# Retention, a rational-gate layer and a gated layer on one core: the steady stages set in program order on every engine

## Chip, core and metric

The kernel runs on one core of a Trainium2 chip. The metric is the device time of one execution in microseconds (us). TensorE is called PE here, VectorE DVE, ScalarE ACT, GpSimd POOL and SyncE SP, as in the profile; PEld is TensorE's loading of weights.

## What is computed

```python
# retention, 4 x 8 heads, 576 positions, 64 wide; gamma per head
ret = (q @ k.T / sqrt(64)) * where(rel >= 0, gamma ** rel, 0)
x = (ret @ v)                       # 2304 tokens x 512
# layer 1: 512 -> 2048 -> 512, a rational gate
h = x @ w_in
P = a[0] + a[1]*h + a[2]*h**2 + a[3]*h**3
Q = 1 + abs(b[0])*abs(h) + abs(b[1])*h**2
x = (P / (Q + 1e-6)) @ w_out
# layer 2: 512 -> 1536 -> 512, rms norm, gated
xn = x / sqrt(mean(x*x) + 1e-6) * rms_g
g, val = xn @ w_gate, xn @ w_val
out = (g * sigmoid(g) * val) @ w_out2
```

The weights come as 64-bit floats. Each float32 factor is split into a high part and a rest, and every product is made of three products of such parts.

## The kernel before

**Head.** The retention, the conversion of layer 1's weights and layer 1's first 18 stages follow a list, `PLAN`, whose order is fixed on every engine by `in_order` (L636): it chains each instruction to the one before it on its engine. What is issued after the list is put in order by a scheduler that works from a modelled timeline.

**Layer 1.** Six tiles of 384 tokens, 16 stages each, one per 128 columns of the hidden width. `s` counts the stages, `n, j = divmod(s, 16)` gives tile and column block. Stage `s` is issued as follows. `m1_up(s)` (L368) makes 12 matmuls into bank 4 or 5. `m1_el` (L466) works on three stages at a time: for `s` ACT makes abs (L403), q (L406) and u (L412), POOL multiplies (`el_qq`, L419), DVE makes `el_p1` and `el_p2` (L423, L427), the last reader of the bank; for `s-1` ACT makes the reciprocal (L434, L439); for `s-2` DVE makes three steps (L443, L447, L452), ACT the high part of the gate's result (`el_gh`, L458) and POOL the rest (`el_gl`, L462). `m1_down(s-3)` (L380) adds the product with w_out into banks 0 to 3: eight matmuls on the high part, then four on the rest (L389).

**Side work in the stages.** A dictionary `late` holds pieces that go ahead of a stage. For the next tile: loads of x and their split (`x_load`, `x_split`, ACT L295 and POOL L299). For the tile that has ended (`be_plan`, L608): the banks are copied out (`be_evac`), squared and added (`be_sq`, L497), summed over partitions by a matmul with ones (`be_sum`, L508), the root is improved by three DVE instructions (`be_newton`, L519), x is scaled by four more (`be_xn`, L528) and stored (`be_out`). In the last tile four `wb.step` calls convert layer 2's weights: on ACT `high` (L194), `scale_hi` (L172), `scale_lo` (L180), on DVE `low` (L198), `shift` (L184), `add` (L190). They stand under `tc.issue_after(mark["el"].ins)`, which keeps them behind the latest activation of the stage.

**Layer 2.** `m2_up(nb, j)` (L539) makes 24 matmuls into banks 4 (gate) and 6 (value); ACT takes the Silu (L552), DVE multiplies (L553), ACT and DVE split the result (L555, L556); `m2_down` (L559) adds three products in each of three banks. Tiles 0 and 1 go side by side while the remaining weights are converted (`step_b`, which also takes a piece of the last tile's norm from the list `norm`), then tiles 2 to 5. With the last `j` the banks are copied out, on DVE, ACT and DVE, and stored through SP's queue (L570 to L574).

**Tables of ACT.** The first activation (L632) is `Abs`; a table is loaded before an activation whose function the active table lacks. Before, there are 7 loads: at L632, twice at L434, three times at L552, once at L513.

Of the kernel before, what the change touches and what calls it, by code (L numbers as in the profile page):

```python
# [12 lines left out]
ACTF = mybir.ActivationFunctionType  # L13
# [63 lines left out]
def retention_moe_kernel(  # L77
# [284 lines left out]


    acc = [b[:, 0:TA] for b in banks[0:KD]]
    g_t, el, el_t, mark = {}, {}, {}, {}
    NS = NA * J1

    def m1_up(s, part=None, b=None):  # L368
# [128 lines left out]
    def be_sq(n, m):  # L497
        if m == 0:
            ss = be_p.tile([128, TA], F32, tag="ss", name="ss")
            be[n] = (be[n], ss)  # L500
            act.activation(out=ss, in_=be[n][0][:, 0], func=ACTF.Square)
        else:
            x2, ss = be[n]
            sq = be_p.tile([128, TA], F32, tag="sq", name="sq")
            act.activation(out=sq, in_=x2[:, m], func=ACTF.Square)
            pool.tensor_tensor(out=ss, in0=ss, in1=sq, op=ALU.add)

    def be_sum(n):  # L508
        x2, ss = be[n]
        pt = banks[6][:, 0:TA]  # L510
        pe.matmul(out=pt, lhsT=ones, rhs=ss, start=True, stop=True)
        y = be_p.tile([128, TA], F32, tag="sq", name="y")
        act.activation(out=y, in_=pt, func=ACTF.Abs_reciprocal_sqrt, scale=1.0 / DM, bias=cst[:, 1:2])  # L513
        dve.tensor_scalar(
            out=ss, in0=pt, scalar1=-0.5 / DM, scalar2=-0.5 * EPS, op0=ALU.mult, op1=ALU.add
        )
        be[n] = (x2, ss, y)

    def be_newton(n):  # L519
        x2, ss, y = be[n]  # L520
        dve.tensor_tensor(out=ss, in0=ss, in1=y, op=ALU.mult)
        dve.tensor_tensor(out=ss, in0=ss, in1=y, op=ALU.mult)
        dve.scalar_tensor_tensor(out=ss, in0=ss, scalar=1.5, in1=y, op0=ALU.add, op1=ALU.mult)
        be[n] = (x2, ss)

    def be_xn(n, m):
        x2, r = be[n]
        dve.scalar_tensor_tensor(  # L528
            out=x2[:, m], in0=x2[:, m], scalar=rg[:, m:m + 1], in1=r, op0=ALU.mult, op1=ALU.mult
        )  # L530

    def be_out(n):
        sp.dma_start(out=xn_d[:, :, n * TA:(n + 1) * TA], in_=be.pop(n)[0])


    y_t = {}
    TT = TB // 128

    def m2_up(nb, j):  # L539
        x = x_t[NA + nb]  # L540
        ps = []
        for kind, b in (("g", 4), ("v", 6)):
            w = wb.got[kind, j]
            t = banks[b][:, 0:TB]
            for k in range(KD):
                ks = slice(k * 128, k * 128 + 128)
                pe.matmul(out=t, lhsT=w[:, 0, ks], rhs=x[:, 0, k], start=(k == 0), stop=False)  # L547
                pe.matmul(out=t, lhsT=w[:, 0, ks], rhs=x[:, 1, k], start=False, stop=False)  # L548
                pe.matmul(out=t, lhsT=w[:, 1, ks], rhs=x[:, 0, k], start=False, stop=(k == KD - 1))  # L549
            ps.append(t)  # L550
        sg = t_p.tile([128, TB], F32, tag="ah", name="sg")
        mark["el"] = act.activation(out=sg, in_=ps[0], func=ACTF.Silu)  # L552
        dve.tensor_tensor(out=sg, in0=sg, in1=ps[1], op=ALU.mult)  # L553
        y = g_p.tile([128, 2, TB], F32R, tag="g", name="y")
        act.activation(out=y[:, 0], in_=sg, func=ACTF.Copy)  # L555
        dve.tensor_tensor(out=y[:, 1], in0=sg, in1=y[:, 0].bitcast(F32), op=ALU.subtract)  # L556
        y_t[nb, j] = y

    def m2_down(nb, j):  # L559
        w, y = wb.got["o", j], y_t.pop((nb, j))  # L560
        for t in range(TT):
            ts = slice(t * 128, t * 128 + 128)
            a = banks[((0, 1, 2), (3, 5, 7))[nb % 2][t]]
            pe.matmul(out=a, lhsT=y[:, 0, ts], rhs=w[:, 0], start=(j == 0), stop=False)  # L564
            pe.matmul(out=a, lhsT=y[:, 0, ts], rhs=w[:, 1], start=False, stop=False)  # L565
            pe.matmul(out=a, lhsT=y[:, 1, ts], rhs=w[:, 0], start=False, stop=(j == J2 - 1))  # L566
            if j == J2 - 1:
                ob = o_p.tile([128, DM], F32, tag="ob", name="ob")
# [163 lines left out]
    x_load(xn_d, 1, 0)  # L732
    x_load(xn_d, 1, 1)
    x_split(NA + 1, 0)
    x_load(xn_d, 1, 2)
    x_split(NA + 1, 1)
    x_load(xn_d, 1, 3)
    m1_down(NS - 2)
# [10 lines left out]
    norm += [lambda: be_sum(NA - 1), lambda: be_newton(NA - 1)]  # L749
    norm += [lambda m=m: be_xn(NA - 1, m) for m in range(KD)]  # L750
    norm += [lambda: be_out(NA - 1)]

    def step_b(eng):
        if norm:
            norm.pop(0)()
        if not norm and len(extra) == 2:
            be_ctx.close()
            extra.extend([new_pool("wr", 2, "right")] * 2)
        if wb.n2 < len(b_order):
            with tc.issue_after(mark["el"].ins):  # L760
                wb.step(eng)

    def next_x(nb, j, j0):
        if nb < NBB and 0 <= j - j0 <= KD:
# [3 lines left out]
                x_load(xn_d, nb, j - j0)  # L768

    for j in range(1, J2):  # L770
        m2_up(0, j)
        if j == J2 - 1:
            o_p = new_pool("ob", 3, "right")
            next_x(2, 0, 0)
            x_load(xn_d, 2, 1)
        step_b(dve)
        m2_down(1, j - 1)
        step_b(dve)
        if j == J2 - 1:
# [4 lines left out]
        m2_up(1, j)  # L784
        step_b(dve)
        m2_down(0, j)
    last = (1, J2 - 1)
    for nb in range(2, NBB):
        for j in range(J2):
            next_x(nb + 1, j, 3)  # L790
            m2_up(nb, j)
            m2_down(*last)
            last = (nb, j)
    m2_down(*last)
# [76 lines left out]
```

## Time and profile before

| | |
|---|---|
| runs shown | 959.3 us median of 3 (957.12 to 961.98) |
| profiled execution, its own time | 957.84 us |
| its span | 956.1 us |
| PE busy | 932.5 us of the span, 5850 matmuls |
| DVE, ACT, POOL busy | 527.5, 530.9, 307.6 us |
| mean DMA rate | 82 GB/s; over 270 GB/s until 125 us |

The profile's page gives these. Matmuls overlap in it: a start follows the last by less than a matmul's own duration, so the distance between starts, not the duration, tells the pace. Of an idle time the view names what ended it.

### The profile page before, as it was taken

How to read it: one execution, taken by the hardware profiler on the slowest of the kernel's cores; microseconds unless marked ns; L12 is line 12 of the kernel's file. 1: busy time of each engine (PE TensorE's matmuls, PEld its weight loads, DVE VectorE, ACT ScalarE, POOL GpSimd, SP SyncE). 2: the span in 40 equal slices, each digit the busy share in tenths (PEclk: the TensorE clock that was granted, in tenths of full speed). 3: DMA queues.
4: the chain of work that ended last, by engine and by line, in shares of the span. 5: the costliest groups of instructions: out<-in, count | busy, mean ns of one | idle time of the engine just before them, and what ended most of it. 6: DMA issues, size and time to landing. Idle time of an engine off the chain costs nothing. (4 is left out here: it accounts for less than half of the span.)

```text
span 956.1 us, 14961 instructions
## 1 busy us (share of the span) xinstructions
PE 932.5 (98%) x5850; PEld 880.7 (92%) x5850; DVE 527.5 (55%) x967; ACT 530.9 (56%) x1030; POOL 307.6 (32%) x293
## 2 busy tenths in 40 slices
PE   7899999999999999999999999999999999999997
PEld 5788889999999999999899899999999999999996
DVE  5989988767767857767865755543112112112111
ACT  3877789779679678788786655533112112111111
POOL 5556756547457466465451000002001001000000
PEclk9999999999999999999999999999999999999999
DMA  9888962001010000010123544403002001000000
GB/s 327 290 280 287 327 204 94 1 34 34 15 36 17 34 25 10 34 34 24 55 86 103 165 132 132 132 31 124 1 1 67 1 1 50 1 1 34 1 1 34
DMA packets 37336, 77.92 MB, mean 82 GB/s; under 512 B 5520, under 2 KB 21008, under 8 KB 37264
## 3 DMA queue, kind: packets, MB, share of 16 engines
q1 hardware_dynamic: 37120, 76.95, 24.2%
q8 instruction: 46, 0.75, 0.3%
q14 instruction: 26, 0.21, 0.1%
q10 hardware_dynamic: 144, 0.01, 0.0%
HBM read 63.57 MB, written 13.37 MB: 80 GB/s over the span
## 5 line engine op out<-in xcount | busy, mean ns | idle before, releaser
L547 PE MATMUL bank<-x,w 128*128 128x384 f32 x528 | 177.0, 336 | 2.7 <-ACT sg L552 1.7
L549 PE MATMUL bank<-x,w 128*128 128x384 f32 x528 | 177.1, 336 | 0.0
L548 PE MATMUL bank<-x,w 128*128 128x384 f32 x528 | 176.8, 335 | 0.0
L553 DVE TENSOR_TENSOR sg<-sg,bank 128x384 f32<-128x384 f32 x72 | 39.9, 554 | 217.5 <-PE bank L549 214.0
L299 POOL TENSOR_TENSOR x<-xr,x 128x384 fp32r<-128x384 f32 x44 | 46.4, 1067 | 289.6 <-ACT x L295 288.3
L376 PE MATMUL bank<-x,w 128*128 128x384 f32 x384 | 131.1, 341 | 7.3 <-DVE u L427 3.0
L552 ACT ACTIVATE sg<-bank 128x384 f32<-128x384 f32 x72 | 35.4, 491 | 180.5 <-PE bank L549 180.5
L385 PE MATMUL bank<-g,w 128*128 128x384 f32 x384 | 129.8, 340 | 0.0
L378 PE MATMUL bank<-x,w 128*128 128x384 f32 x384 | 129.1, 336 | 0.0
L377 PE MATMUL bank<-x,w 128*128 128x384 f32 x384 | 128.9, 336 | 0.0
L386 PE MATMUL bank<-g,w 128*128 128x384 f32 x384 | 127.9, 334 | 0.0
L419 POOL TENSOR_TENSOR q<-q,ah 128x384 f32<-128x384 f32 x88 | 91.0, 1034 | 95.5 <-ACT q L406 92.7
L547 PEld LDWEIGHTS bank<-x,w 128*128 128x128 f32 x528 | 99.1, 188 | 6.5 <-ACT sg L552 2.1
L462 POOL TENSOR_TENSOR g<-u,g 128x384 fp32r<-128x384 f32 x80 | 82.7, 1035 | 59.8 <-issue 40.5
L548 PEld LDWEIGHTS bank<-x,w 128*128 128x128 f32 x528 | 99.1, 188 | 2.7
L549 PEld LDWEIGHTS bank<-x,w 128*128 128x128 f32 x528 | 99.1, 188 | 0.1
L555 ACT ACTIVATE y<-sg 128x384 fp32r<-128x384 f32 x72 | 37.6, 522 | 101.7 <-DVE sg L553 101.7
L423 DVE TENSOR_TENSOR u<-u,bank 128x384 f32<-128x384 f32 x96 | 52.9, 551 | 62.4 <-ACT u L412 60.5
L389 PE MATMUL bank<-g,w 128*128 128x384 f32 x384 | 86.7, 338 | 0.0
L376 PEld LDWEIGHTS bank<-x,w 128*128 128x128 f32 x384 | 72.4, 188 | 11.4 <-DVE u L427 4.7
L434 ACT ACTIVATE bank<-q,cst 128x384 f32<-128x384 f32 x96 | 56.0, 584 | 41.4 <-POOL q L419 34.9
L385 PEld LDWEIGHTS bank<-g,w 128*128 128x128 f32 x384 | 72.2, 188 | 1.2
(99 smaller groups left out, 1905.1 us busy)
## 6 DMA issues: line engine op xcount, KB each, us to landing
raw<-in_w_out_dram SPq DMA_DIRECT2D x28, 512.0 KB, 3.6
xb<-in_qkT_dram SPq DMA_DIRECT2D x16, 512.0 KB, 6.8
kv<-in_kv_dram SPq DMA_DIRECT2D x16, 512.0 KB, 6.1
raw<-in_w_in_dram SPq DMA_DIRECT2D x16, 512.0 KB, 5.4
raw<-in_w_gate_dram SPq DMA_DIRECT2D x12, 512.0 KB, 4.3
raw<-in_w_val_dram SPq DMA_DIRECT2D x12, 512.0 KB, 3.5
xn_d<-x SPq DMA_DIRECT2D x6, 768.0 KB, 3.8
xr<-xn_d SPq DMA_DIRECT2D x24, 192.0 KB, 2.4
```

The source lines that it names most:

```text
L376: pe.matmul(out=h, lhsT=w[:, 0, ks], rhs=x[:, 0, k], start=(k == 0), stop=False)
L377: pe.matmul(out=h, lhsT=w[:, 0, ks], rhs=x[:, 1, k], start=False, stop=False)
L378: pe.matmul(out=h, lhsT=w[:, 1, ks], rhs=x[:, 0, k], start=False, stop=(k == KD - 1))
L385: pe.matmul(out=acc[m], lhsT=w[:, 0, ms], rhs=g[:, 0], start=(j == 0), stop=False)
L386: pe.matmul(out=acc[m], lhsT=w[:, 1, ms], rhs=g[:, 0], start=False, stop=False)
L389: pe.matmul(out=acc[m], lhsT=w[:, 0, ms], rhs=g[:, 1], start=False, stop=(j == J1 - 1))
L419: eng.tensor_tensor(out=q, in0=q, in1=el_t[i]["ah"], op=ALU.mult)
L434: act.activation(out=el[i], in_=el_t[i]["q"], func=ACTF.Abs_reciprocal_sqrt, bias=cst[:, 0:1])
L462: eng.tensor_tensor(out=g[:, 1], in0=el_t[i]["r"], in1=g[:, 0].bitcast(F32), op=ALU.subtract)
L547: pe.matmul(out=t, lhsT=w[:, 0, ks], rhs=x[:, 0, k], start=(k == 0), stop=False)
L548: pe.matmul(out=t, lhsT=w[:, 0, ks], rhs=x[:, 1, k], start=False, stop=False)
L549: pe.matmul(out=t, lhsT=w[:, 1, ks], rhs=x[:, 0, k], start=False, stop=(k == KD - 1))
```

## The change

The stages from `S0` on are issued in the order in which the program lists them, on every engine, up to the last `j` of layer 2's first two tiles (`in_order(pinned)`), and once more for the last `m2_down`. A second dictionary, `done`, holds pieces that go behind a stage's `m1_el` instead of ahead of it: the splits of x, the squares, the Newton step, the scalings of x (one a stage) and the store. `tc.issue_after` is gone. `be_sum` is cut in two, the matmul and `be_root`. Layer 2's first x tile is loaded and split ten stages earlier. `m2_up` is cut into matmuls (`m2_mm`) and the rest (`m2_el`), and the very first value product goes to bank 5 instead of 6, so that all of tile 0's first product can stand ahead of layer 1's last three `m1_down`. The last tile's sum and root move to a fixed place in `j == 2`. The first activation asks for the reciprocal root's table. The last 128 rows of the output are copied and stored in two halves, by ACT and ACT's queue and by DVE and SP's.

```diff
@@ be_sum
         pe.matmul(out=pt, lhsT=ones, rhs=ss, start=True, stop=True)
+        be[n] = (x2, ss, pt)
+
+    def be_root(n):
+        x2, ss, pt = be[n]
         y = be_p.tile([128, TA], F32, tag="sq", name="y")
@@ m2_up
-    def m2_up(nb, j):
+    def m2_mm(nb, j):
-        for kind, b in (("g", 4), ("v", 6)):
+        for kind, b in (("g", 4), ("v", 6 if nb + j else 5)):
...
+        mm_t[nb, j] = ps
+
+    def m2_el(nb, j):
+        ps = mm_t.pop((nb, j))
...
@@ m2_down
+                r0 = nb * TB + t * 128
+                if nb == NBB - 1 and t == TT - 1:
+                    h = DM // 2
+                    act.activation(out=ob[:, 0:h], in_=a[:, 0:h], func=ACTF.Copy)
+                    dve.tensor_copy(out=ob[:, h:], in_=a[:, h:])
+                    act.dma_start(out=out[r0:r0 + 128, 0:h], in_=ob[:, 0:h])
+                    sp.dma_start(out=out[r0:r0 + 128, h:], in_=ob[:, h:])
+                    continue
@@ x_plan
-            late.setdefault(s0 + k + 1, []).insert(0, lambda k=k: x_split(to, k))
+            at(s0 + k + 1, lambda k=k: x_split(to, k), done)
@@ be_plan
         for m in range(KD):
-            at(s + 2 + m, lambda m=m: be_sq(n, m))
-            at(s + 9 + m, lambda m=m: be_xn(n, m))
-        at(s + 7, lambda: be_sum(n))
-        at(s + 8, lambda: be_newton(n))
-        at(s + 13, lambda: be_out(n))
+            at(s + 2 + m, lambda m=m: be_sq(n, m), done)
+            at(s + 8 + m, lambda m=m: be_xn(n, m), done)
+        at(s + 7, lambda: (be_sum(n), be_root(n)))
+        at(s + 7, lambda: be_newton(n), done)
+        at(s + 11, lambda: be_out(n), done)
@@ first activation
-    act.activation(out=qb, in_=cst, func=ACTF.Abs)
+    act.activation(out=qb, in_=cst, func=ACTF.Abs_reciprocal_sqrt)
@@ the stages
-    x_plan(NS - 6, xn_d, 0, NA)
-
+    x_plan(NS - J1, xn_d, 0, NA)
+
+    pinned = len(traced)
     for s in range(S0, NS):
...
         m1_up(s)
         m1_el(s)
-        if n == NA - 1 and j in (6, 9, 12, 15):
-            with tc.issue_after(mark["el"].ins):
-                wb.step(dve)
-        if s >= LAG:
-            m1_down(s - LAG)
+        for f in done.pop(s, []):
+            f()
+        if n == NA - 1 and j in (6, 10, 12, 14):
+            wb.step(dve)
+        m1_down(s - LAG)
...
+    m2_mm(0, 0)
+    x_load(xn_d, 1, 0)
+    x_load(xn_d, 1, 1)
     m1_el(NS)
-    m2_up(0, 0)
+    x_split(NA + 1, 0)
...
     m1_down(NS - 3)
     m1_el(NS + 1)
...
+    m2_el(0, 0)
     x_split(NA + 1, 2)
     x_split(NA + 1, 3)
+    wb.step(dve)
+    m1_down(NS - 2)
     m1_down(NS - 1)
     be_evac(NA - 1)
+    m2_mm(1, 0)
     wb.step(dve)
-    m2_up(1, 0)
-    wb.step(dve)
+    m2_el(1, 0)
     m2_down(0, 0)
...
     for j in range(1, J2):
-        m2_up(0, j)
+        m2_mm(0, j)
+        m2_el(0, j)
         if j == J2 - 1:
+            in_order(pinned)
...
+        if j == 2:
+            m2_down(0, j)
+            be_sum(NA - 1)
+            be_root(NA - 1)
         step_b(dve)
-        m2_down(0, j)
+        if j == 1:
+            wb.step(dve)
+        if j != 2:
+            m2_down(0, j)
...
+    pinned = len(traced)
+    m2_down(*prev)
+    in_order(pinned)
```

Two places show how instructions move. The first is DVE in the last tile of layer 1, around the scaling of the tile before it. There `u` is the polynomial, `q` the denominator, `x_4795` and `x_4808` the tile that is scaled, `ft`, `raw` and `w` a weight in conversion. Before:

```order
L423 TENSOR_TENSOR u<-u,bank_101 128x384
L447 SCALAR_TENSOR_TENSOR bank_103<-q,bank_103 128x384
L452 SCALAR_TENSOR_TENSOR u<-u,cr,bank_104 128x384
L528 SCALAR_TENSOR_TENSOR x_4795<-x_4795,cr,ss 128x384 x4
L427 SCALAR_TENSOR_TENSOR u<-u,cr,bank_101 128x384
L452 SCALAR_TENSOR_TENSOR u<-u,cr,bank_103 128x384
```

In the change (L532 is the scaling):

```order
L423 TENSOR_TENSOR u<-u,bank_101 128x384
L427 SCALAR_TENSOR_TENSOR u<-u,cr,bank_101 128x384
L532 SCALAR_TENSOR_TENSOR x_4808<-x_4808,cr,ss 128x384
L198 TENSOR_TENSOR w<-ft,w 128x512
L184 TENSOR_SCALAR ft<-ft 128x512
L190 ISA ft<-raw,ft 128x1024
L443 SCALAR_TENSOR_TENSOR q<-q,bank_104 128x384
L447 SCALAR_TENSOR_TENSOR bank_104<-q,bank_104 128x384
L452 SCALAR_TENSOR_TENSOR u<-u,cr,bank_104 128x384
```

The four scalings no longer stand between a bank's two last readers (L423 and L427); one follows them. The weight's three instructions now stand between L427 and the next L443.

The second place is ACT where layer 2 begins (`sg` the Silu, `g` the gate's high part, `x<-xr` the split of x). Before:

```order
L552 ACT_TABLE_LOAD
L552 ACTIVATE sg<-bank_101 128x384
L458 ACTIVATE g<-u 128x384
L434 ACT_TABLE_LOAD
L434 ACTIVATE bank_104<-q,cst 128x384
L180 ACTIVATE raw<-raw 128x512
L194 ACTIVATE w<-ft 128x512
L439 ACTIVATE bank_104<-bank_104 128x384
L295 ACTIVATE x<-xr 128x384
L172 ACTIVATE ft<-raw 128x512
L295 ACTIVATE x<-xr 128x384
```

In the change:

```order
L458 ACTIVATE g<-u 128x384
L560 ACT_TABLE_LOAD
L560 ACTIVATE sg<-bank_101 128x384
L563 ACTIVATE y<-sg 128x384
L295 ACTIVATE x<-xr 128x384 x2
L194 ACTIVATE w<-ft 128x512
L172 ACTIVATE ft<-raw 128x512
L180 ACTIVATE raw<-raw 128x512
```

The Silu's table is loaded once, behind layer 1's last gate, where before the two tables took turns; over the whole program the loads go from 7 to 4 (L647, L560, L517, L560).

## Rows read from the trace of the kernel before

**Rows 1.** The page, part 1: busy time, share and instructions of each engine
```profile
PE 932.5 (98%) x5850; PEld 880.7 (92%) x5850; DVE 527.5 (55%) x967; ACT 530.9 (56%) x1030; POOL 307.6 (32%) x293
```

**Rows 2.** Waits of PE, longest first: total us, times, longest us
```profile
PE bank L376 <- DVE u L427: 3.0, 3, 2.1
...
PE bank L547 <- ACT sg L552: 1.7, 1, 1.7
...
PE bank L547 <- DVE sg L553: 1.0, 1, 1.0
```

**Rows 3.** Timeline of PE around the longest wait: start us, duration, [idle before]
```profile
466.07 0.34 PE L378 MATMUL bank<-x,w 128*128 128x384 f32 x1
468.53 0.45 PE L376 MATMUL bank<-x,w 128*128 128x384 f32 x1 [2.12 <-DVE u L427]
```

**Rows 4.** Sums by stretch: busy us (instructions) of each engine, granted PE clock, DMA
```profile
150.00:250.00 100.00, 100.00 (x576) 99.41 (x575) 73.59 (x136) 81.75 (x166) 61.50 (x62) 1.00 0.11 35
...
468.50:472.40 3.90, 3.87 (x13) 3.86 (x14) 2.29 (x5) 2.85 (x7) 2.21 (x3) 0.58 0.56 202
```

**Rows 5.** Groups by shape, 200 to 250 us, ACT: busy us, mean ns | idle before
```profile
L406 ACT ACTIVATE q<-ah,qb 128x384 f32<-128x384 f32 x12 | 8.5, 706 | 0.0
L412 ACT ACTIVATE u<-bank,ncf 128x384 f32<-128x384 f32 x12 | 8.1, 671 | 0.0
...
L434 ACT ACTIVATE bank<-q,cst 128x384 f32<-128x384 f32 x12 | 7.0, 585 | 6.0 <-POOL q L419 5.9
...
L403 ACT ACTIVATE ah<-bank 128x384 f32<-128x384 f32 x13 | 6.4, 491 | 2.0 <-PE bank L378 1.9
L458 ACT ACTIVATE g<-u 128x384 fp32r<-128x384 f32 x12 | 6.3, 526 | 0.8 <-DVE u L452 0.6
L439 ACT ACTIVATE bank<-bank 128x384 f32<-128x384 f32 x12 | 5.8, 485 | 0.1
```

**Rows 6.** Timeline of ACT, DVE and POOL, 457 to 469 us
```profile
457.77 0.62 ACT L194 ACTIVATE w<-ft 128x512 fp32r<-128x512 f32 x1
...
458.07 1.03 POOL L462 TENSOR_TENSOR g<-u,g 128x384 fp32r<-128x384 f32 x1
458.29 0.66 ACT L172 ACTIVATE ft<-raw 128x512 f32<-128x512 f32 x1
458.42 1.23 DVE L198 TENSOR_TENSOR w<-ft,w 128x512 fp32r<-128x512 f32 x1
458.86 0.67 ACT L180 ACTIVATE raw<-raw 128x512 int32<-128x512 uint32 x1
...
460.90 0.68 DVE L190 CUSTOM_DVE_ANT_0 ft<-raw,ft 128x1024 uint16<-128x1024 uint16 x1
...
465.76 2.19 DVE L528 SCALAR_TENSOR_TENSOR x<-x,cr,ss 128x384 f32<-128x384 f32 x4
```

**Rows 7.** Timeline of ACT where layer 2 begins
```profile
493.21 1.28 ACT L552 ACT_TABLE_LOAD   x1
494.50 0.49 ACT L552 ACTIVATE sg<-bank 128x384 f32<-128x384 f32 x1
```

**Rows 8.** Timeline of DVE, 532 to 540 us
```profile
535.17 2.21 DVE L528 SCALAR_TENSOR_TENSOR x<-x,cr,ss 128x384 f32<-128x384 f32 x4
537.29 0.68 DVE L198 TENSOR_TENSOR w<-ft,w 128x512 fp32r<-128x512 f32 x1
```

**Rows 9.** Timeline of all engines, 31 to 39 us
```profile
31.52 1.28 ACT L434 ACT_TABLE_LOAD   x1
...
34.01 0.43 DVE L184 TENSOR_SCALAR ft<-ft 128x512 int32<-128x512 int32 x1 [1.07 <-ACT ft L172]
...
35.33 1.09 PE L324 MATMUL bank<-ret,kv 128*64 128x128 f32 x16 [1.51 <-DVE xe L333]
```

**Rows 10.** The end: timelines of DVE and SP, and the stores of L574
```profile
950.11 1.29 DVE L570 COPY ob<-bank 128x512 f32<-128x512 f32 x2 [1.94 <-PE bank L566]
...
950.83 1.30 SPq L574 DMA_DIRECT2D out_dram<-ob  x3
...
DMA to landing us min/median/max: 2.0/2.8/4.1
```

More of the change, by code (lines that the diff above doesn't have):

```diff
@@ L364, in retention_moe_kernel @@
     acc = [b[:, 0:TA] for b in banks[0:KD]]
-    g_t, el, el_t, mark = {}, {}, {}, {}
+    g_t, el, el_t = {}, {}, {}
     NS = NA * J1
@@ L411, in el_u @@
     def el_u(i):
-        mark["el"] = act.activation(
+        act.activation(
             out=el_alloc(i, "u"), in_=el[i], func=ACTF.Identity,
@@ L533, in be_out @@
         sp.dma_start(out=xn_d[:, :, n * TA:(n + 1) * TA], in_=be.pop(n)[0])
-    y_t = {}
+    y_t, mm_t = {}, {}
     TT = TB // 128
-    def m2_up(nb, j):
+    def m2_mm(nb, j):
         x = x_t[NA + nb]
         ps = []
-        for kind, b in (("g", 4), ("v", 6)):
+        for kind, b in (("g", 4), ("v", 6 if nb + j else 5)):
             w = wb.got[kind, j]
@@ L550, in m2_up @@
             ps.append(t)
+        mm_t[nb, j] = ps
+    def m2_el(nb, j):
+        ps = mm_t.pop((nb, j))
         sg = t_p.tile([128, TB], F32, tag="ah", name="sg")
-        mark["el"] = act.activation(out=sg, in_=ps[0], func=ACTF.Silu)
+        act.activation(out=sg, in_=ps[0], func=ACTF.Silu)
         dve.tensor_tensor(out=sg, in0=sg, in1=ps[1], op=ALU.mult)
@@ L572, in m2_down, with at @@
                     act.activation(out=ob, in_=a, func=ACTF.Copy)
-                r0 = nb * TB + t * 128
                 sp.dma_start(out=out[r0:r0 + 128, :], in_=ob)
-    late = {}
-    def at(s, f):
-        late.setdefault(s, []).append(f)
+    late, done = {}, {}
+    def at(s, f, when=late):
+        when.setdefault(s, []).append(f)
     xr = {}
@@ L717, in retention_moe_kernel @@
         m1_el(s)
-        if n == NA - 1 and j in (6, 9, 12, 15):
-            with tc.issue_after(mark["el"].ins):
-                wb.step(dve)
-        if s >= LAG:
-            m1_down(s - LAG)
-            if (s - LAG) % J1 == J1 - 1:
-                be_plan((s - LAG) // J1, s)
+        for f in done.pop(s, []):
[3 more added lines that the diff above has]
+        m1_down(s - LAG)
+        if (s - LAG) % J1 == J1 - 1:
+            be_plan((s - LAG) // J1, s)
+    m2_mm(0, 0)
+    x_load(xn_d, 1, 0)
+    x_load(xn_d, 1, 1)
     m1_el(NS)
-    m2_up(0, 0)
+    x_split(NA + 1, 0)
+    x_load(xn_d, 1, 2)
+    x_split(NA + 1, 1)
+    x_load(xn_d, 1, 3)
     m1_down(NS - 3)
@@ L731, in retention_moe_kernel @@
     extra += [new_pool("wl", 2)] * 2
[L732 to L738, printed above, removed]
+    m2_el(0, 0)
     x_split(NA + 1, 2)
     x_split(NA + 1, 3)
+    wb.step(dve)
+    m1_down(NS - 2)
     m1_down(NS - 1)
     be_evac(NA - 1)
+    m2_mm(1, 0)
     wb.step(dve)
-    m2_up(1, 0)
-    wb.step(dve)
+    m2_el(1, 0)
     m2_down(0, 0)
     norm = [lambda m=m: be_sq(NA - 1, m) for m in range(KD)]
-    norm += [lambda: be_sum(NA - 1), lambda: be_newton(NA - 1)]
+    norm += [lambda: None, lambda: None, lambda: be_newton(NA - 1)]
     norm += [lambda m=m: be_xn(NA - 1, m) for m in range(KD)]
@@ L759, in step_b @@
         if wb.n2 < len(b_order):
-            with tc.issue_after(mark["el"].ins):
-                wb.step(eng)
+            wb.step(eng)
     def next_x(nb, j, j0):
@@ L783, in retention_moe_kernel @@
                     x_load(xn_d, 2, k + 2)
-        m2_up(1, j)
-        step_b(dve)
-        m2_down(0, j)
-    last = (1, J2 - 1)
+        m2_mm(1, j)
+        m2_el(1, j)
+        if j == 2:
+            m2_down(0, j)
+            be_sum(NA - 1)
+            be_root(NA - 1)
+        step_b(dve)
+        if j == 1:
+            wb.step(dve)
+        if j != 2:
+            m2_down(0, j)
+    prev = (1, J2 - 1)
     for nb in range(2, NBB):
@@ L790, in retention_moe_kernel @@
             next_x(nb + 1, j, 3)
[L791 to L794, printed above, removed]
+            m2_mm(nb, j)
+            m2_el(nb, j)
+            m2_down(*prev)
+            prev = (nb, j)
+    pinned = len(traced)
+    m2_down(*prev)
+    in_order(pinned)
 _OUT = ((NT, DM), "float32")
```

## The prediction

> **What bounds the kernel now.** I read the busy shares first: PE works in 98% of the span, every other engine in 56% or less [rows 1]. The reader is to see that only PE's gaps can be won. Next the sums by stretch: in layer 1 PE is busy 100.00 of 100 us with 576 matmuls, so one is worth 0.1736 us and a stage of 24 is 4.17 us; ACT is at 82% there, DVE at 74% [rows 4]. Then the list of PE's waits, which holds what is left to win behind the head: 3.0 us in three waits where `m1_up` needs a bank whose last reader, L427, is late; 1.7 us at layer 2's second product, which needs the bank that the Silu still reads; 1.0 us for the multiply L553 [rows 2].
>
> The timelines tell why. The longest of the three falls in layer 1's last tile: PE starts a matmul at 466.07 and the next at 468.53 [rows 3]. On DVE the four scalings L528 run from 465.76 for 2.19 us [rows 6], and the order shows that they stand between a bank's two last readers. [...] The 1.7 us is ACT loading a table for 1.28 us before the first Silu [rows 7]. The 1.0 us is four scalings again (2.21 us) and a weight's `low` ahead of the multiply [rows 8]. Head and end are fixed lists and stores and come below.
>
> **The change, part by part.**
>
> *Waits removed.* The five waits sum to 5.7 us [rows 2]. A wait costs more than its idle time: start to start the longest lost 2.46 - 0.17 = 2.29 us for an idle time of 2.12 [rows 3], and its first matmul takes 0.45 us instead of 0.34, so 0.17 + 0.11 = 0.28 on top; for five waits 1.4. The slow clock costs 3.9 - 13 x 0.1736 = 1.64 us [rows 4], in which one 0.11 is counted. Together 5.7 + 1.4 + 1.64 - 0.1 = **8.6 us**. I take all of it away, because each cause is moved: the scalings come one a stage and behind L427; the tables are loaded once; tile 0's first product has three `m1_down` (6.2 us) behind it to cover the Silu's table and the rest of the gate.
>
> *Is a pinned stage short enough?* ACT is what I checked: six instructions a stage, 0.71 + 0.67 + 0.59 + 0.49 + 0.53 + 0.49 = 3.46 us [rows 5], the gate's high part last. PE wants that part when the next stage's `m1_up` is through, 4.17 us after the bank was ready, or about 4.0 since matmuls overlap. That leaves 0.5 us; a split or a square (about one more L458) comes behind it and still fits. The two bank copies at a tile's start also fit into the 0.7 us that is free. So ordinary stages should wait for nothing, in all four inner tiles.
>
> *Wait added: the weight steps of layer 1's last tile.* Four `wb.step` calls go there (j = 6, 10, 12, 14), and now the queue behind them is fixed. ACT makes the three activations after the stage's six: 3.46 + 0.62 + 0.66 + 0.67 = 5.4 us; DVE's `add` (0.68) can only follow, to 6.1 [rows 5, 6]. Behind it in DVE's queue stand L443, L447 and L452 of the next gate. DVE's mean instruction is 73.59 / 136 = 0.54 us [rows 4], each needs the last one's result, so some 1.75 us: 7.85; then ACT's high part 0.53: 8.4. PE wants it at 4.17 + 4.0 = 8.17. So each of the three full steps is late by 0.2 us at least. At most it is late by that, by one blocked DVE instruction (L198 took 1.23 us instead of 0.68 while POOL ran: 0.55 [rows 6, 8]) and by a Newton step or a scaling that came ahead (0.55 each): 1.3. I take 0.9 each, nearer the upper end, since at j = 10 and 12 a scaling does stand ahead; after j = 14 it is L427 of the last stage that is late, for the value product in bank 5. With 0.1 for each restart: **+3.0 us**, between 0.9 and 4.2. Behind this nothing else is queued that PE needs at once; the splits of layer 2's second x tile run while PE makes the three `m1_down`, and their loads (SP) come behind one weight load.
>
> *Layer 2's first two tiles.* On ACT a pair of products (2 x 6.25 us of PE) has two Silus, two splits and three weight steps of 0.62 + 0.66 + 0.67, about 8 us of 12.5, and some 2.5 us in which ACT now stands in its queue waiting for the multiply. It fits. The root's two table loads (2 x 1.28) fall behind `m2_down` in `j == 2` with half a pair of slack. I take nothing; if that cover is gone, the cost is the 1.28 of one load.
>
> *The head's table.* The load at 31.52 goes to the start, where ACT waits for data anyway. Behind it ACT's L172 was late, so DVE waited 1.07 us for it, and PE 1.51 us for the DVE instruction after [rows 9]. At most 1.07 us comes back, at least nothing, since the head streams weights throughout and a later transfer may swallow it. I take **-0.5**. [...]
>
> *The end.* PE's end is unchanged, but the first bank is complete earlier, so DVE is free when the last bank comes. Its copy ended at 951.40 (two of 0.65 [rows 10]); two halves of about 0.4 after the last matmul end near 951.0. The three stores are issued 0.43 us apart by SP; the last now is two, on two queues. A store took 2.0 to 4.1 us to land [rows 10]: with the slow value nothing is won, with the fast one 2.0 us. I take **-0.9**, one copy's and one issue's worth, because the stores before it still share the queue.
>
> *Sum.* -8.6 + 3.0 - 0.5 - 0.9 = -7.0 us against the profiled execution's own 957.84 (span 956.1 and 1.7 around it): 950.8, say **951**. That execution lies 1.5 under the median of the runs shown, 959.3, so runs around 952 would be the same result.
>
> **The rivals.**
>
> *The queues absorb the steps.* If DVE's instructions slip between POOL's and the step's end is hidden, the +3.0 falls away: 950.8 - 3.0 = 947.8. For it: the smallest lateness is 0.2 us a step. Against: DVE then has 5 x 0.54 + 0.55 + 0.68 + 0.42 + 0.68 = 5.0 us of work in a stage of 4.17.
>
> *DVE and POOL collide.* The pinned queues put `low`, `add` and the scalings, which read two tiles of SBUF, right beside POOL's `el_gl`. Ten such instructions in the last tile at 0.55 each are 5.5 us instead of the 0.9 to 1.2 I have in the sum; an idle time near 2 us brings the slow clock back (1.6). That gives 950.8 + 3 + 1.6 = 955.4. For it: 1.23 against 0.68 [rows 6, 8]; against: the layer's steady DVE instructions read banks and show no such stretch. [...]
>
> *Slower: the ACT chain is longer than the stage.* The high part now always comes last of six. If waits between them stretch 3.46 us beyond 4.0, every one of 78 stages pays: at 0.2 us each 15.6 us, or 966. It decides at 0.1 us a stage, where the 7 us are gone. For it: the scheduler used another order on ACT and still had it at 82%. Against: abs, q and u wait for nothing but each other, and DVE has 26% free.
>
> *Waits only move.* A pinned order can lose as much elsewhere, at a tile's start or in layer 2: about 957.8.
>
> **How the numbers follow.** My forecast 0.50 (its own range 949 to 953.5); absorbed 0.24; collisions 0.15; chain 0.06; moved 0.05. A measurement of this kernel can tell about 0.5%, 4.8 us, so faster means below 954.5: 0.48 + 0.24 + 0.05 = 0.77. Same: most of the collisions and of the moved waits, 0.17. Slower: 0.06. The range leaves out the chain and part of the moved: from 946.5 (absorbed, with the upper bounds of head and end) to 957.
>
> **What would show it.** Right: PE's list of waits behind 150 us no longer has L427 in the four inner tiles, nor a Silu; a few short waits of 0.3 to 1.3 us stand between 470 and 500 us, for ACT's L458 and for L427; the granted clock stays 1.00; ACT has 4 table loads; PE's last matmul starts some 6 to 8 us earlier and the span's end follows by about 0.9 less. Wrong: waits for L458 in ordinary stages (the chain), a granted clock under 1 after 470 us (collisions), or PE's waits in the first 150 us grown.

## The result, and the profile after

| | before | after |
|---|---|---|
| median of the runs | 958.92 us (6 runs, 957.12 to 961.98) | 950.05 us (6 runs, 948.96 to 952.91) |
| ratio, 95% interval | | 0.9910 (0.9889 to 0.9932) |
| profiled execution: own time, span | 957.84, 956.1 us | 951.18, 949.4 us |
| PE's last matmul starts at | 950.14 us | 945.25 us |
| ACT table loads | 7 | 4 |

The changed kernel is 0.9% faster; 951.0 was predicted. The busy shares of the page answer to [rows 1]:

```profile
PE 932.0 (98%) x5850; PEld 879.7 (93%) x5850; DVE 551.7 (58%) x967; ACT 535.6 (56%) x1028; POOL 311.6 (33%) x293
```

The list of what PE waited for (engine, line, total us, times, longest) answers to [rows 2]:

```profile
PE bank L385 <- ACT g L458: 1.6, 2, 0.8
...
PE bank L551 <- DVE u L427: 0.9, 1, 0.9
```

The waits for L427 in four tiles, for the Silu and for the multiply L553 are gone. The new waits stand in layer 1's last tile, where the prediction put them: behind the weight steps of j = 10 and j = 12 for L458, and behind that of j = 14 for L427. PE's timeline at the first of them answers to [rows 3]:

```profile
468.86 0.34 PE L378 MATMUL bank<-x,w 128*128 128x384 f32 x1
470.00 0.45 PE L385 MATMUL bank<-g,w 128*128 128x384 f32 x1 [0.80 <-ACT g L458]
```

Start to start it lost 1.14 - 0.17 = 0.97 us, and 0.11 in its first matmul. Counted so, each with its slower first matmul, the three waits cost 3.3 us. Three smaller ones bring it to 4.2: 0.36 behind the step of j = 6, 0.20 at the last tile's bank copies and 0.26 early in layer 2. The sums around the first wait answer to the slow stretch of [rows 4]; the granted clock is 1.00 where it was 0.58:

```profile
468.50:472.40 3.90, 3.10 (x19) 2.78 (x18) 3.79 (x7) 3.05 (x7) 2.32 (x3) 1.00 0.43 134
```

DVE is busy 3.79 of the 3.90 us. Its timeline before the wait says why (start us, duration, instruction, [idle before]):

```profile
459.17 0.61 DVE L427 SCALAR_TENSOR_TENSOR u<-u,cr,bank 128x384 f32<-128x384 f32 x1
459.70 0.55 DVE L525 TENSOR_TENSOR ss<-ss,y 128x384 f32<-128x384 f32 x1
460.29 1.25 DVE L526 TENSOR_TENSOR ss<-ss,y 128x384 f32<-128x384 f32 x1
...
464.87 1.04 DVE L532 SCALAR_TENSOR_TENSOR x<-x,cr,ss 128x384 f32<-128x384 f32 x1
465.83 0.68 DVE L198 TENSOR_TENSOR w<-ft,w 128x512 fp32r<-128x512 f32 x1
466.44 0.42 DVE L184 TENSOR_SCALAR ft<-ft 128x512 int32<-128x512 int32 x1
466.99 0.69 DVE L190 CUSTOM_DVE_ANT_0 ft<-raw,ft 128x1024 uint16<-128x1024 uint16 x1
467.60 0.55 DVE L443 SCALAR_TENSOR_TENSOR q<-q,bank 128x384 f32<-128x384 f32 x1
```

No row has an idle time: the Newton step of j = 9, the scaling and the weight step follow each other with no break over 0.14 us. `add` (L190) was not held up by ACT, whose third activation of that step had ended at 466.05; nor was it at j = 12 (475.43, `add` at 476.41) or at j = 14 (484.86, 485.36). Two rows are long. L525 and L526 are the same operation on the same shape, 0.55 and 1.25 us; the scaling takes 1.04. POOL in the same stretch:

```profile
460.03 1.09 POOL L462 TENSOR_TENSOR g<-u,g 128x384 fp32r<-128x384 f32 x1 [0.95 <-ACT g L458]
...
464.48 1.02 POOL L462 TENSOR_TENSOR g<-u,g 128x384 fp32r<-128x384 f32 x1 [1.23 <-ACT g L458]
```

Both long instructions overlap POOL's L462 (g's low part), and each ends 0.4 us behind it. So after the result there were two theories for the 3.3 us: `add` waits for ACT (the forecast), or DVE has too much work, part of it stretched by POOL. All five L526 and all twenty scalings L532 of the steady part are long (mean 1249 and 1231 ns):

```profile
L532 DVE SCALAR_TENSOR_TENSOR x<-x,cr,ss 128x384 f32<-128x384 f32 x20 | 24.6, 1231 | 0.0
...
L526 DVE TENSOR_TENSOR ss<-ss,y 128x384 f32<-128x384 f32 x5 | 6.2, 1249 | 0.2
```

### The profile page after: what moved, and what is told of

It is laid out like the page before. It is cut to its first block, busy times and chain, and to the rows that moved or that the text cites. A ratio compares the mean times of both kernels' runs of the same rounds, so it can differ in the third digit from the quotient of the medians.

```text
span 949.4 us, 14895 instructions
## 1 busy us (share of the span) xinstructions
PE 932.0 (98%) x5850; PEld 879.7 (93%) x5850; DVE 551.7 (58%) x967; ACT 535.6 (56%) x1028; POOL 311.6 (33%) x293
## 5 line engine op out<-in xcount | busy, mean ns | idle before, releaser
L553 PE MATMUL bank<-x,w 128*128 128x384 f32 x528 | 177.2, 336 | 0.0
L299 POOL TENSOR_TENSOR x<-xr,x 128x384 fp32r<-128x384 f32 x44 | 49.3, 1125 | 263.4 <-ACT x L295 263.4
L560 ACT ACTIVATE sg<-bank 128x384 f32<-128x384 f32 x72 | 35.1, 487 | 145.6 <-PE bank L553 145.6
L419 POOL TENSOR_TENSOR q<-q,ah 128x384 f32<-128x384 f32 x88 | 91.1, 1035 | 77.0 <-ACT q L406 73.7
L462 POOL TENSOR_TENSOR g<-u,g 128x384 fp32r<-128x384 f32 x80 | 81.6, 1020 | 81.3 <-POOL q L419 44.6
L553 PEld LDWEIGHTS bank<-x,w 128*128 128x128 f32 x528 | 99.1, 188 | 0.0
L423 DVE TENSOR_TENSOR u<-u,bank 128x384 f32<-128x384 f32 x96 | 52.9, 551 | 57.0 <-ACT u L412 55.6
L403 ACT ACTIVATE ah<-bank 128x384 f32<-128x384 f32 x96 | 47.0, 490 | 51.3 <-PE bank L378 50.6
```

The lines of the kernel that those rows point to most:

```text
L419: eng.tensor_tensor(out=q, in0=q, in1=el_t[i]["ah"], op=ALU.mult)
L423: dve.tensor_tensor(out=u, in0=u, in1=el[i], op=ALU.mult)
L462: eng.tensor_tensor(out=g[:, 1], in0=el_t[i]["r"], in1=g[:, 0].bitcast(F32), op=ALU.subtract)
```

## The experiments

**A yardstick.** The changed kernel once more.

> The changed kernel once more, as the yardstick for the other kernels on the same chip: 950 us, PE's last matmul starting near 945.2, waits of 0.8 + 0.8 + 0.9 us for L458 (twice) and L427 between 468 and 488 us.

Measured: 951.0 us median (949.57 to 951.8), ratio 0.9915 (0.9900 to 0.9931), with the same three waits at 0.80, 0.80 and 0.90 us. The trace gives a finer ruler than the medians. All kernels issue 5,850 matmuls, so starts of matmuls of the same number can be compared: the 1526th (layer 1 is steady there), the 3001st (ahead of the last tile's first waits), the 3601st (layer 2 is steady) and the last. Each row below is one execution, times in us.

| kernel | median | start of 1526th | 1526 to 3001 | 3001 to 3601 | 3601 to last | span's end less last |
|---|---|---|---|---|---|---|
| before | 958.9 | 150.09 | 259.00 | 111.94 | 429.11 | 5.91 |
| changed | 950.05 | 150.03 | 256.87 | 110.15 | 428.20 | 4.15 |
| changed, again | 951.0 | 148.41 | 256.87 | 110.15 | 428.21 | 4.15 |
| changed, free order | 981.4 | 150.40 | 261.02 | 131.27 | 431.93 | 5.10 |
| before, pinned | 969.1 | 152.16 | 256.87 | 126.01 | 429.27 | 5.01 |
| DVE's half deferred | 956.2 | 148.81 | 256.87 | 115.64 | 428.27 | 4.16 |
| `low` on POOL | 953.6 | 148.51 | 256.88 | 113.02 | 428.22 | 4.16 |
| steps spread | 949.6 | 148.99 | 256.87 | 108.82 | 428.20 | 4.16 |
| spread, two tiles | 949.7 | 151.22 | 256.88 | 108.82 | 428.20 | 4.15 |
| scalings in the gap | 948.8 | 149.62 | 256.87 | 108.35 | 428.20 | 4.14 |
| all in the gap | 947.8 | 150.92 | 256.87 | 107.04 | 428.20 | 4.15 |
| old ends | 951.6 | 150.82 | 256.88 | 110.15 | 428.20 | 4.12 |
| value in bank 6 | 951.4 | 148.01 | 256.87 | 111.28 | 428.20 | 4.16 |

Where the order is pinned the stretches repeat to 0.01 us; the head does not, it spreads over 4 us. The two executions of the changed kernel differ by 1.6 us, and all of it is in the head; that the medians differ for the same reason is likely, but only these two are traced. The stretch from the 3001st to the 3601st matmul, where layer 1 ends and layer 2 begins, is called the seam below.

**Text or pin?** The change does two things: it rewrites the program's order, and it makes each engine keep that order (`in_order`). Each was run without the other.

```
@@ the changed kernel, free order @@
         if j == J2 - 1:
-            in_order(pinned)
...
-    pinned = len(traced)
     m2_down(*prev)
-    in_order(pinned)
@@ the kernel before, pinned @@
+    pinned = len(traced)
     for s in range(S0, NS):
...
         if j == J2 - 1:
+            in_order(pinned)
...
```

> The changed kernel without the pinned order (both in_order calls behind the head are gone); the scheduler again orders the steady stages of both layers. Theory (the order by itself removes the waits): the four scalings stand in one group on DVE again, ACT loads tables 6 times, waits for L427 of 0.4 to 2 us come back at the starts of tiles and the Silu's wait of over 1 us too; 954 to 958 us. Rival (the rearranged steps do it, the pinning is idle): 950 us, and no L427 wait in the four inner tiles.

Measured: 981.42 us, ratio 1.0231 (1.0212 to 1.0250). The theory's side held, its size did not: 23 us slower than before, where it ended at 958. PE's list of waits:

```profile
PE bank L376 <- DVE u L427: 8.3, 9, 1.7
PE bank L385 <- ACT g L458: 7.5, 5, 5.7
PE bank L551 <- ACT sg L560: 3.6, 4, 2.0
```

The 5.7 us stands at 478 us. DVE's timeline there shows the four scalings in one block again, with n1 and p1 of different gates and parts of two weight steps behind it:

```profile
476.95 3.26 DVE L532 SCALAR_TENSOR_TENSOR x<-x,cr,ss 128x384 f32<-128x384 f32 x4
480.13 0.41 DVE L184 TENSOR_SCALAR ft<-ft 128x512 int32<-128x512 int32 x1
480.47 0.55 DVE L447 SCALAR_TENSOR_TENSOR bank<-q,bank 128x384 f32<-128x384 f32 x1
480.94 0.54 DVE L443 SCALAR_TENSOR_TENSOR q<-q,bank 128x384 f32<-128x384 f32 x1
481.40 0.54 DVE L423 TENSOR_TENSOR u<-u,bank 128x384 f32<-128x384 f32 x1
481.86 0.68 DVE L198 TENSOR_TENSOR w<-ft,w 128x512 fp32r<-128x512 f32 x1
```

The rewritten text by itself is worse than the old one. It also dropped the `issue_after` notes of the old one; how much is due to that was not tried, nor were the parts of the rewrite tried one by one.

> The kernel before, its program text unchanged but for the pinned order of the steady stages (in_order over both layers, the last tile's down product left free). Theory (pinning needs the rearrangement): the waits for L427 in the three inner tiles go (1 to 3 us), but the weight steps at j = 6, 9, 12, 15 make DVE late as in the changed kernel, and the second product's value half waits for bank 6 until n3 of the last gate has read it (about 3.5 us), perhaps with a slow clock behind it; 953 to 958 us. Rival (pinning alone is the gain): 950 to 951 us with no wait over 1 us behind 460 us.

Measured: 969.08 us, ratio 1.0108 (1.0088 to 1.0127): slower than before, though the theory had 958 as its end. The table splits it. In the inner tiles the pin alone gives the whole gain, 256.87 for 259.00. At the seam of the layers it costs 14 us; PE's list of waits:

```profile
PE bank L385 <- ACT g L458: 4.6, 2, 2.4
PE bank L547 <- DVE u L452: 3.7, 1, 3.7
...
PE bank L547 <- ACT x L295: 1.4, 1, 1.4
```

The 3.7 us is the value product waiting in bank 6 for n3 of the last gate but one, as expected. The two waits for L458 (2.41 and 2.21 us) are larger than in the changed kernel. Ahead of the first, a weight step and the whole Newton step stand in one row on DVE (461.8 to 466.4 us); ahead of the second, POOL also has a split of layer 2's x (at 480.1 us L190 took 1.54, at 481.6 a scaling 1.36). Behind each the granted clock fell, and 13 matmuls were made in 3.9 us, by the sums of these stretches:

```profile
468.70:472.60 3.90, 3.84 (x13) 3.84 (x14) 3.79 (x7) 3.61 (x9) 3.26 (x3) 0.57 0.10 29
485.20:489.10 3.90, 3.86 (x13) 3.86 (x14) 3.79 (x7) 3.44 (x7) 3.28 (x3) 0.57 0.30 108
```

The last row is at 512 us: PE waits for the split of layer 2's second x tile, whose loads land late, then 0.63 us more for POOL's part of it (L299). Over the whole span the granted clock was 0.988 in this execution, for 0.997 in the kernel before. So at the seam the two parts need each other. The 2.1 us of the inner tiles are the pin's alone, and so, as the ends show below, is part of the tail.

**Is it `add` that waits?** DVE's part of each weight step was moved one stage behind ACT's, so that nothing on DVE waits for ACT.

```
         if n == NA - 1 and j in (6, 10, 12, 14):
-            wb.step(dve)
+            half = wb.step_act()
+        if n == NA - 1 and j in (7, 11, 13, 15):
+            wb.step_dve(*half, dve)
...
```

`step_act` makes `high`, `scale_hi` and `scale_lo`; `step_dve` makes `low`, `shift` and `add` and issues the next load.

> The changed kernel, with DVE's part of each weight step in layer 1's last tile (low, shift, add, load) one stage behind ACT's part (high, scale_hi, scale_lo). Theory (DVE's queue stands behind `add`, which waits for ACT's last activation of the stage): the waits for L458 and L427 of 0.8 + 0.8 + 0.9 us and the small ones go, in all some 3.9 us with restarts, of which a little may come back where DVE has 5 us of work in a 4.17 us stage; 946 to 947.5 us, PE's last matmul near 941.5 to 943. Rival (DVE simply has too much work in those stages, or it collides with POOL): the waits stay and move one stage later, 950 us, within 1 us of the changed kernel.

Measured: 956.23 us (12 runs), ratio 0.9974 (0.9963 to 0.9985); the seam grew by 5.5 us. Neither text foresaw that, and the forecast's theory falls: with `add` waiting for nothing, the waits more than doubled (4.2 + 5.5 us). DVE's timeline behind stage j = 11 (this kernel's lines stand 16 further down: L548 is the scaling, L474 to L478 the gate's g, L435 POOL's q):

```profile
468.24 0.61 DVE L548 SCALAR_TENSOR_TENSOR x<-x,cr,ss 128x384 f32<-128x384 f32 x1
468.76 1.51 DVE L198 TENSOR_TENSOR w<-ft,w 128x512 fp32r<-128x512 f32 x1
470.20 1.23 DVE L184 TENSOR_SCALAR ft<-ft 128x512 int32<-128x512 int32 x1
471.47 0.69 DVE L190 CUSTOM_DVE_ANT_0 ft<-raw,ft 128x1024 uint16<-128x1024 uint16 x1
```

And POOL's:

```profile
468.63 1.10 POOL L478 TENSOR_TENSOR g<-u,g 128x384 fp32r<-128x384 f32 x1 [1.01 <-POOL q L435]
469.91 1.24 POOL L435 TENSOR_TENSOR q<-q,ah 128x384 f32<-128x384 f32 x1 [0.18 <-ACT q L422]
```

`low` (L198) takes 1.51 us for 0.68, `shift` (L184) 1.23 for 0.42, each while POOL is in an instruction of its own. What the deferral moved was not a wait but a place in time, and the new place was beside POOL.

**Less work for DVE.** One instruction of each step was given to POOL.

```
         if n == NA - 1 and j in (6, 10, 12, 14):
-            wb.step(dve)
+            wb.step(pool)
```

> The changed kernel with one instruction of each weight step in layer 1's last tile (`low`, 0.68 us) on POOL instead of DVE. Theory A (DVE's work): the waits for L458 at 468.9 and 478.3 us and for L427 at 487.7 us fall by about 0.7 us each, to 0 to 0.3 us; about 948 us. Theory B (`add` waits for ACT): they stay at 0.8 to 0.9 us, 950 us. A third case: POOL, with about 3.4 us of work in such a stage, makes DVE's two-input instructions longer or its own q late, and the waits grow: 951 us or more.

Measured: 953.57 us, ratio 0.9943 (0.9927 to 0.9959); the third case. The waits at j = 10 and 12 went from 0.80 to 1.92 and 1.91 us. DVE's timeline behind j = 10:

```profile
463.37 1.04 DVE L532 SCALAR_TENSOR_TENSOR x<-x,cr,ss 128x384 f32<-128x384 f32 x1
464.34 1.51 DVE L184 TENSOR_SCALAR ft<-ft 128x512 int32<-128x512 int32 x1
465.99 1.31 DVE L190 CUSTOM_DVE_ANT_0 ft<-raw,ft 128x1024 uint16<-128x1024 uint16 x1
```

And POOL's:

```profile
462.98 1.02 POOL L462 TENSOR_TENSOR g<-u,g 128x384 fp32r<-128x384 f32 x1 [1.23 <-ACT g L458]
463.95 1.62 POOL L198 TENSOR_TENSOR w<-ft,w 128x512 fp32r<-128x512 f32 x1
465.74 1.02 POOL L419 TENSOR_TENSOR q<-q,ah 128x384 f32<-128x384 f32 x1 [0.16 <-ACT q L406]
```

DVE has 0.68 us less to do, and its other two instructions of the step take 2.82 us instead of 1.11. This shows the collision by itself: same instructions, same operands, only POOL's company differs. The shift ends 0.3 us behind POOL's L198 and L190 0.5 us behind L419; what makes them longer beside POOL no row tells. DVE's instructions that read a bank were not stretched: L427 and L452 take 0.61 us in this kernel too, beside POOL or not.

**Steps away from scalings.**

```
-        if n == NA - 1 and j in (6, 10, 12, 14):
+        if s in (NS - 17, NS - 15, NS - 12, NS - 10):
             wb.step(dve)
...
-    x_plan(NS - J1, xn_d, 0, NA)
+    x_plan(NS - 7, xn_d, 0, NA)
```

> The changed kernel with the four weight steps of layer 1's last tile moved away from its Newton steps and scalings: one into the last stage of the tile before, the others to j = 1, 4 and 6; the loads and splits of layer 2's first x tile move from j = 0 to 4 to j = 9 to 13 to make room on ACT. Theory A (DVE has more work than a stage holds where a step meets a Newton step or a scaling): no wait over 0.4 us is left between 425 and 500 us, PE's last matmul 3 to 3.9 us earlier, 946 to 947 us. Theory B (as forecast: each step costs since `add` waits for ACT's last activation): every step brings its wait of 0.2 to 1.0 us along to its new place, 949 to 950.5 us.

Measured: 949.60 us, ratio 0.9901 (0.9885 to 0.9918), inside the range of theory B; the seam is 1.3 us shorter, between the theories. The waits at j = 10, 12 and 14 went, and two steps brought one along: 0.48 us at 429 and 0.86 us at 451 us. On DVE's timeline the steps of j = 4 and j = 6 differ in little but POOL:

```profile
438.69 0.74 DVE L198 TENSOR_TENSOR w<-ft,w 128x512 fp32r<-128x512 f32 x1 [1.14 <-ACT w L194]
439.35 0.41 DVE L184 TENSOR_SCALAR ft<-ft 128x512 int32<-128x512 int32 x1
...
447.36 0.73 DVE L198 TENSOR_TENSOR w<-ft,w 128x512 fp32r<-128x512 f32 x1 [1.14 <-ACT w L194]
448.01 1.24 DVE L184 TENSOR_SCALAR ft<-ft 128x512 int32<-128x512 int32 x1
```

The first, uncollided, made PE wait 0.13 us (at 442.9); the second, beside POOL's L506 (at 447.5 us, 1.47 long), 0.86 us. Both show a wait of DVE for ACT too, 1.14 us ahead of `low`, where the forecast had it ahead of `add`: it is real, but alone it made PE wait only 0.13 us.

**Another place in the stage.** DVE waits 1.2 us for ACT's u between n3 and p1 in an ordinary stage. The scalings were put there, first by themselves, then with the spread steps and DVE's half of each.

```
             el_n3(s - 2)
+        for f in gap.pop(s, []):
+            f()
...
-            at(s + 8 + m, lambda m=m: be_xn(n, m), done)
+            at(s + 8 + m, lambda m=m: be_xn(n, m), gap)
@@ all in the gap, added to the spread steps @@
-            wb.step(dve)
+            half = wb.step_act()
+            at(s + 1, lambda half=half: wb.step_dve(*half, dve), gap)
```

> The changed kernel with the scalings (be_xn) placed on DVE between n3 and p1, where DVE waits 1.2 us for ACT's u in an ordinary stage, instead of behind p2, where POOL is in its gl. Collision theory: a scaling takes 0.6 us there instead of 1.04 to 1.09, so DVE gets back 0.45 us in each of the stages j = 10 to 13; the wait at j = 10 falls from 0.80 to about 0.35 us, those at j = 12 and behind j = 14 to 0 to 0.5 us; 1.5 to 2 us less between layer 1's last tile's start and layer 2's first product, 948 to 949 us. Rival (it is the number of DVE's instructions and the wait of `add` for ACT): the waits stay at 0.8 us, 950 to 951 us. A miss of another kind: p1 and p2 come later and L376 waits for L427.

Measured: 948.82 us, ratio 0.9898 (0.9875 to 0.9921); the seam 1.80 us shorter, inside the 1.5 to 2 expected. The wait at j = 10 is 0.37 us, at j = 12 none, behind j = 14 0.46 us. The scaling of j = 10 on DVE:

```profile
463.38 0.61 DVE L534 SCALAR_TENSOR_TENSOR x<-x,cr,ss 128x384 f32<-128x384 f32 x1
463.91 0.55 DVE L423 TENSOR_TENSOR u<-u,bank 128x384 f32<-128x384 f32 x1
```

0.61 us, as POOL's L462 starts at 464.10 only. So it is with all four of the last tile (460 to 480 us: busy us, mean ns); one of an earlier tile stands below them:

```profile
L534 DVE SCALAR_TENSOR_TENSOR x<-x,cr,ss 128x384 f32<-128x384 f32 x4 | 2.4, 612 | 0.0
...
200.51 1.41 DVE L534 SCALAR_TENSOR_TENSOR x<-x,cr,ss 128x384 f32<-128x384 f32 x1
```

In the changed kernel the four took 4.3 us. DVE's instructions are the same in number, it got back 1.9 us, and the seam got 1.8 us shorter: it was the collision. But the gap is not free of POOL: in each earlier tile the third and the fourth scaling took 1.4 us there, beside POOL's q product L419. DVE has time in those tiles, and their stretch stayed 256.87 us.

> The spread weight steps of the earlier experiment, with the scalings and DVE's half of each weight step (low, shift, add) between n3 and p1 (for the weight steps in the following stage). Theory: DVE's extra work fills the 1.2 us in which it waits for ACT's u, n3 comes on time in every stage, and no wait of PE over 0.3 us is left between 425 and 500 us; the last tile is 2 us shorter than with the spread steps alone and 3.5 us shorter than in the changed kernel, 946.5 to 947.5 us. Rival (POOL's q product, which runs in the same gap, collides instead): `low` and `shift` take 1.2 us there and L376 waits for L427; 949 us or more.

Measured: 947.84 us (945.37 to 948.97), ratio 0.9888 (0.9866 to 0.9909), 0.3 us above the expected range; the seam is 3.11 us shorter than in the changed kernel and 1.78 shorter than with the spread steps. PE's list has no wait for L474 (L458 of the other kernels) or L443 (its L427) any more; its longest behind 425 us is 0.11 us. The rival's collisions came in part, one `low` of 1.22 us and two scalings of 1.37 and 1.42 us, but with the steps spread DVE had room for them. This kernel beats both, by 3 us of the seam; the medians say 2.2 to 3.2 us, with intervals that overlap the changed kernel's.

**The ends.** Both ends of the change undone:

```
-    act.activation(out=qb, in_=cst, func=ACTF.Abs_reciprocal_sqrt)
+    act.activation(out=qb, in_=cst, func=ACTF.Abs)
...
-                if nb == NBB - 1 and t == TT - 1:
...
```

> The changed kernel with both of its ends as before: the first activation is Abs (so the rsqrt table is loaded later, in the head), and the last 128 rows are evacuated by one copy and one store. Forecast of the terms: head 0 to 1.07 us and end 0.9 us, so 951 to 952.5 us. By the changed kernel's own trace the end was worth 1.8 us (span's end less PE's last matmul 4.15 for 5.9 us) and the head nothing (the matmul near 148.7 us started at the same time): then span's end less last matmul is again 5.5 to 6 us and the matmul near 148.7 us stays within 0.3 us, 951.8 us.

Measured: 951.63 us, ratio 0.9922 (0.9907 to 0.9937). The tail did not come back: 4.12 us from the last matmul to the span's end, as with the split halves (4.15). So neither of my two values was right; the split is worth nothing here. What is worth something shows on PE. Its timeline at the end of the kernel before:

```profile
948.98 0.39 PE L565 MATMUL bank<-wx,y 128*128 128x512 f32 x1
949.21 0.39 PE L564 MATMUL bank<-wx,y 128*128 128x512 f32 x1
949.45 0.39 PE L565 MATMUL bank<-wx,y 128*128 128x512 f32 x1
949.68 0.86 PE L566 MATMUL bank<-wx,y 128*128 128x512 f32 x3
```

And of this run:

```profile
944.65 0.39 PE L574 MATMUL bank<-wx,y 128*128 128x512 f32 x1
...
945.35 0.39 PE L574 MATMUL bank<-wx,y 128*128 128x512 f32 x1
...
946.05 0.40 PE L574 MATMUL bank<-wx,y 128*128 128x512 f32 x1
```

L566 and L574 are the matmul that completes a bank. The scheduler put the three side by side, so all banks came at once and copies and stores queued; pinned, they come 0.70 us apart. The two kernels whose last `m2_down` was not pinned, one of them with the split, have tails of 5.10 and 5.01 us, the pinned ones 4.12 to 4.16. That is 0.9 us of the gain. The other 0.9 up to the 5.91 of before is its last store, which took 3.4 us to land; it took 2.6 and 2.5 in those two. One execution of each doesn't show that this part would come again. The head did not repeat well enough to price the table load (0.6 us above the second median of the changed kernel and 1.6 above the first, with intervals that overlap).

> The kernel with the spread weight steps, and the two halves of the last evacuation in two tiles instead of one, so that DVE's half need not stand behind ACT's. Theory (the two halves are ordered because they share a tile): DVE's half starts beside ACT's, 0.4 us earlier, and the span's end less PE's last matmul goes from 4.15 to about 3.75 us; 0.4 us under the kernel with the spread steps alone, 945.5 to 946.7 us. Rival (it is the store behind that sets the end): no difference.

```
-                    dve.tensor_copy(out=ob[:, h:], in_=a[:, h:])
+                    o2 = t_p.tile([128, TB], F32, tag="ah", name="o2")
+                    dve.tensor_copy(out=o2[:, 0:h], in_=a[:, h:])
...
-                    sp.dma_start(out=out[r0:r0 + 128, h:], in_=ob[:, h:])
+                    sp.dma_start(out=out[r0:r0 + 128, h:], in_=o2[:, 0:h])
```

Measured: 949.70 us, ratio 0.9901 (0.9883 to 0.9920), tail 4.15. DVE's half still starts only when ACT's has ended:

```profile
945.98 0.42 DVE L582 COPY o<-bank 128x256 f32<-128x256 f32 x1 [1.13 <-ACT ob L580]
```

The tile was not the tie. The two halves still share the bank that both read; that this is the tie was not tried.

**A run that measured something else.** One part undone, `b = 6` for the value product of layer 2's first tile (`("v", 6)`).

> The changed kernel with one part undone: the value product of layer 2's first tile goes into bank 6, as before, and not into bank 5. Bank 6 is read by the last gate but one until its n3, which in the changed kernel ends at 490.6 us, L427 of the last gate (bank 5) at 488.9 us: PE's wait there grows from 0.92 to about 2.6 us. Theory: 1.7 us longer, and if the clock falls behind it as it fell behind the 2.12 us of the kernel before, 1.6 us more: 3000th to 3600th matmul 111.9 to 113.5 us instead of 110.15, 951.8 to 953.5 us. Rival (the three m1_down behind the product give the time back, since the gate's reader was late anyway): no difference, 110.15 us.

Measured: 951.35 us, ratio 0.9923 (0.9898 to 0.9948), the seam 1.13 us longer. It doesn't price the bank: the new text issues the product ahead of the last gates' n steps, so in bank 6 its sums take the place of y of the last gate but one, which these steps then read. No wait for n3 can arise there, and none did; the time went into a wait for that gate's L458 (0.44 us) and others. Bank 5 belongs to the new order and can't be taken out of it alone.

## Why the prediction was right

- **Waits removed, -8.6.** From the 1526th to the last matmul the profiled execution gained 2.13 + 1.79 + 0.91 = 4.83 us net, and the new waits cost 4.2, so 9.0 went. Counted one by one, start to start, the waits for L427 in four tiles, for the Silu and for L553, with the slow clock behind the longest, come to 9.0 as well, for 8.6 in the forecast. Of that 2.1 lies in the inner tiles and is the pin's alone.
- **An ordinary stage is short enough.** Right: 256.87 us for 1475 matmuls in every pinned kernel, no wait for L458 there. The bank copies did not quite fit at the last tile's start (0.20 us).
- **Waits added, +3.0.** Places right; 3.7 measured (the three waits and the one behind j = 6), inside my 0.9 to 4.2. But the step that carried the number was wrong: "DVE's `add` (0.68) can only follow, to 6.1". At j = 10, 12 and 14 `add` waited for nothing from ACT; at j = 10 DVE was full, with a whole Newton step of the stage before (2.4 us, where the forecast had one instruction of 0.55) and two instructions stretched by 0.70 and 0.44 us. Taking the wait for ACT away made it worse by 5.5 us. The rival "DVE and POOL collide" named the cause, as part of DVE's load. It had ten stretched instructions, 5.5 us, and the slow clock: seven came in the last tile (L526, the four scalings, one `add` of 1.26 us and one `low` of 1.15), 3.6 us longer together, and the clock stayed at 1.00. The deferral that follows from the forecast's reason gives back 5 to 6 of the 9 us that the change won.
- **Head, -0.5.** Not seen. The 1526th matmul starts at 150.03 for 150.09; the 1.5 us wait of [rows 9] fell to 0.3, and others grew. Over 13 executions that start lies anywhere from 148.0 to 152.2.
- **End, -0.9.** 1.8 measured (5.91 to 4.15), near the far end of its bounds of 0 and 2.0, and half of it is one slow store before. "PE's end is unchanged, but the first bank is complete earlier" was the working part; the two halves brought nothing; the second waits for the first.
- **Sum.** -4.8 - 0.1 - 1.8 = -6.7 us of span, for -7.0. That they agree to 0.3 us is luck in part: 1.2 us more in added waits and 0.4 less from the head were nearly made up by 0.9 more at the end and 0.4 more in waits removed. The medians fell by 8.9 us, and by 7.6 in the second measurement.

## What to carry to other kernels

Pin an order and write it in the same step: each alone made this kernel slower. When an engine is near full in a stage, ask of each added instruction not only how long it takes but what the neighbour does meanwhile; DVE's instructions on SBUF operands (here a scaling of 0.61 us took 1.04 to 1.41 beside POOL) belong where POOL is idle, and the gap in which DVE waits for another engine is better than the place behind the last of its chain, since there a stretched instruction (1.4 us for 0.6) can still cost nothing. Compare versions over a fixed run of matmuls in the trace: it told the 108.35 us of one kernel's seam from the 108.82 of another, whose runs overlap (947.76 to 949.31 and 948.83 to 950.04 us).

## What was not expected of the hardware

- Collisions reach beyond instructions with two SBUF inputs: the shift L184 with one took, for 0.42 us, 1.23 with DVE's half deferred, 1.24 with the steps spread and 1.54 with `low` on POOL (mean of three), and POOL's own instruction grew too (L435 1.24 us for 1.02 with DVE's half deferred; L198 1.62 at j = 10 with `low` on POOL, where the median of POOL's 23 in the changed kernel is 1.29).
- After idle times of 0.8 us, and of 1.92 and 1.91 us in the run with `low` on POOL, PE's granted clock stayed 1.00 (22 matmuls in 3.9 us behind each of the last two); after 2.12 us in the kernel before, and after 2.41 and 2.21 us in that kernel pinned, it was 0.58 and 0.57 over 3.9 us from the restart (in the kernel before 1.00 in the first 0.5 us and 0.50 from 469.2 to 472.4). After the 5.7 us of the run with free order it was 0.50 over 3.9 us, with 12 matmuls.
